# C of block 2 loaded by head pairs and turned on VectorE, the decay rows read back earlier, late stores whole

## The chip, the cores and the metric

One core of one Trainium2 chip runs the kernel. The metric is the device time of one execution in microseconds (us). The kernel before took 123.31 us in the median of three runs (123.02 to 123.41).

Five engines run their own instruction queues in order and meet through semaphores: TensorE (PE) multiplies matrices, VectorE (DVE), ScalarE (ACT) and GpSimd (POOL) work on tensors, and SyncE (SP) issues most of the transfers between memory (DRAM) and the chip's own SBUF. ACT and POOL issue some transfers too. PE writes to PSUM, which has eight banks.

## The reference, cut to what matters

A state-space scan (4 batches, 8 heads, 768 tokens, head size 32, state size 16) feeds a bilinear feed-forward layer.

```python
# per chunk of tokens, per batch and head; cum = running sum of log a within the chunk
M       = (C @ B.T) * exp(cum_i - cum_j) * causal          # tokens x tokens
y       = M @ x + (C @ state) * exp(cum_i)
state   = exp(sum log a) * state + sum_j B_j x_j exp(cum_end - cum_j)
# then, with the 8 heads side by side (256 wide):
out     = ((y @ w_a) * (y @ w_b)) @ w_out                  # 3072 x 256, f32
```

## The kernel before, in words

**Tiling.** The 768 tokens make six blocks of 128. Two batches with all their heads make a pair; a block has two pairs, so pairs 0 to 11 stand in the order of blocks, and pair p belongs to block p // 2. B and C are loaded in f32, scaled by decay factors of their tokens (a running product of `a`, over its value at the middle of the block) and cast to f16. The factor for C is that ratio, the factor for B its reciprocal, so that C @ B.T already has the decay in it.

**One pair.** `scale_bc` (L370) scales B or C of one pair on POOL, result `bm` or `cm`. `transposes` (L386) turns both to state-by-token form on PE (L409, into a PSUM bank `tr`); ACT copies B out twice (L413, `bt`) and C once (L425, `ct`). `scores` (L437) multiplies them, `mask` (L490) applies the causal mask (three quarters of a pair on DVE, L497; one quarter copied by ACT, L494, and masked by POOL, L495). `scale_x` (L357) casts x. `pv` (L555, pairs 2 and 3) or `outputs` (L583, whole blocks from block 2 on) multiplies with x and adds the state's part; `state_sums` (L646, DVE) and `state_spread` (L658, POOL: L662 or L670, then L677) carry the state from block to block.

**The other way for C.** For blocks 3 to 5 (`by_block`, L142, through `NT = 3`) C is not loaded by pairs. `load_block` (L179) issues eight transfers of 32 KB on SP, one for each of eight heads, so that four tokens of one head stand in a row of 256 bytes: tile `rq`. `scale_block` (L188) scales all four batches in one POOL instruction (L191, `mq`), and `turn_pair` (L199) turns one pair's share on DVE by 32x32 blocks (L202, `tq`). B of block 5 goes the same way. The pair loads (`load2`, L170, L174) move 128 KB in one transfer with 64 bytes in a row.

**Their factors.** `late_rows` (L319) makes the decay rows `Ps` on DVE; `store_rows` (L332, L334 on SP) writes them to DRAM, and `spread_rows` (L337, four transfers of POOL, L339) reads them back into the partitions that `load_block` uses (`Pq`); `block_factors` (L344, L345 on DVE) turns them into `fCq`. The pair-wise factors of the late blocks come straight from `Ps` by `late_factors` (L328, L330) and `fb(2)` (L826).

**The feed-forward layer.** For pairs 0 to 3, `unit(p, k)` (L726) does two of twelve slices: Wa matmuls (`aps`), a copy by ACT (`asb`, L715), Wb matmuls (`bps`), and the product on DVE (`times`, L722, `hk`). `out_half` (L755) multiplies with `w_out` (L737), ACT scales and SP stores. Whole blocks use `bunit` (L761; L769, L779) and `bout` (L785; L794, L806, stores L809 and L811).

**The order of work** is written out by hand, from L840 to the end, and each engine takes its instructions in that order. Four PSUM banks are passed around by a string, `BANKS` (L22): each call of `bank` takes the next digit, so the string says which earlier result must have been read before PE may write. The other four banks, `SC`, hold scores and pair results.

Around the change, the order is: scores of pair 2 with the state spread of pair 1 (L952); POOL then scales pair 3's B and C, reads the rows back (L971) and casts x of pair 3; the second half of pairs 0 and 1's output; transposes of pair 3; scores of pair 3 (L1030); the loads of pairs 4 to 11 on SP; units of pair 2; `pv(3)`; `block_factors` (L1048); transposes of pairs 4 and 5 (L1050, L1054), with the state sums of pair 3 and half outputs between; the scores of pairs 4 and 5 with units of pair 3; `group(2)`, block 2's outputs, and transposes of pairs 6 and 7.

Of the kernel before, what the change touches and what calls it, by code (L numbers as in the profile page):

```python
# [10 lines left out]
f32 = mybir.dt.float32  # L11
# [8 lines left out]
YS = 16.0  # L20

BANKS = (  # L22
    "0123102031203123012301230123102310231023102310231023102130213012301230210321302103123021"
    "0321032103123012032103201231023102310213201320312031203120312031203120312031203120312031"
    "2031"
)


# [1 line left out]
def kernel(  # L30
# [13 lines left out]
    nc = tc.nc  # L44

    nb, H, S, D = x.shape
    N = B.shape[-1]
    Q = 128
    NBLK = S // Q
# [5 lines left out]
    NBP = nb // 2  # L55
    NP = NBP * NBLK
    NG = NBLK - 1
    P0 = 4
    NT = 3


    j = np.arange(128)
# [21 lines left out]
    big = ctx.enter_context(tc.tile_pool(name="big", bufs=1))  # L84
# [19 lines left out]
    selr = big.tile([BH, 2, NBP, H], f32, name="selr")  # L104
    NL = NBLK - P0 // NBP
    Ps = big.tile([BH, NL, Q], f32, name="Ps")
    fBl = big.tile([128, NL, NBP * 2 * H], f32, name="fBl")
    fCl = big.tile([128, NL, NBP * 2 * H], f32, name="fCl")
    Pq = big.tile([128, NT, Q], f32, name="Pq")
    fCq = big.tile([128, NT, 4, 32], f32, name="fCq")  # L110
    fBq = big.tile([128, 4, 2 * nb], f32, name="fBq")
# [2 lines left out]
    hsx = big.tile([128, nb, NG], f32, name="hsx")  # L114
    G = big.tile([128, nb, NG], f32, name="G")

    inp = ctx.enter_context(tc.tile_pool(name="inp", bufs=9))
    pre = ctx.enter_context(tc.tile_pool(name="pre", bufs=6))
    mid = ctx.enter_context(tc.tile_pool(name="mid", bufs=4))
    ffh = ctx.enter_context(tc.tile_pool(name="ffh", bufs=4))  # L120
# [17 lines left out]
    def bank(name):  # L138
        return psf.tile([128, 512], f32, name=name, tag=f"ff{next(banks)}")


    def by_block(blk, which):  # L142
        return blk >= NBLK - NT and (which == 1 or blk == NBLK - 1)

# [32 lines left out]
        )  # L177

    def load_block(eng, blk, which):  # L179
        raw = inp.tile([128, nb, 2, 4, N], f32, name="rq", tag="rq", bufs=3)  # L180
        st[("raw", blk, which)] = raw
        for m, e in itertools.product(range(4), range(2)):
            eng.dma_start(
                raw[32 * m : 32 * m + 32, :, e].rearrange("i b g n -> i b (g n)"),
                (B, C)[which][:, 2 * m + e, blk * Q : (blk + 1) * Q, :].rearrange("b (i g) n -> i b (g n)", g=4),
            )

    def scale_block(blk, which, eng):  # L188
        f = fCq[:, blk - (NBLK - NT), :, 0 : 2 * nb] if which else fBq
        m_ = pre.tile([128, 4, nb, 2, N], f16, name="mq", tag="mq", bufs=2)  # L190
        eng.tensor_tensor(  # L191
            out=m_.rearrange("p g b e n -> p (b e) g n"),
            in0=st[("raw", blk, which)].rearrange("p b e g n -> p (b e) g n"),
            in1=f.rearrange("p g j -> p j g").unsqueeze(3).broadcast_to((128, 2 * nb, 4, N)),
            op=ALU.mult,
        )
        st[("scaled", blk, which)] = m_

    def turn_pair(p, which):  # L199
        blk, bp = divmod(p, NBP)  # L200
        t_ = mid.tile([128, 2, Q], f16, name="tq", tag="tq", bufs=6)
        nc.vector.transpose(  # L202
            t_.rearrange("p t (i g) -> p g t i", g=4),
            st[("scaled", blk, which)][:, :, 2 * bp : 2 * bp + 2].rearrange("p g t e n -> p g t (e n)"),
        )
        st[("turned", p, which)] = t_
        if which:
            st.setdefault(p, {})["CT"] = t_
# [116 lines left out]
    def last_factors():  # L325
        nc.vector.reciprocal(fBq, fCq[:, NT - 1, :, 0 : 2 * nb])

    def late_factors():  # L328
        for c0 in range(0, Q, 32):
            nc.vector.transpose(fCl[c0 : c0 + 32], Ps[:, :, c0 : c0 + 32])  # L330

    def store_rows(eng):  # L332
        rows = far.tile([BH, NT, Q], f32, name="rows")
        eng.dma_start(rows, Ps[:, NL - NT :])  # L334
        return rows

    def spread_rows(eng, rows):  # L337
        for m in range(4):
            eng.dma_start(  # L339
                Pq[32 * m : 32 * m + 2 * nb],  # L340
                rows.rearrange("(b h) k q -> b h (k q)", h=H)[:, 2 * m : 2 * m + 2],
            )

    def block_factors():  # L344
        nc.vector.transpose(  # L345
            fCq.rearrange("p k g j -> p (k g) j"), Pq.rearrange("p k (i g) -> p k g i", g=4)
        )
# [310 lines left out]
    def state_spread(p):  # L658
        blk, bp = divmod(p, NBP)
        if p + NBP < P0:  # L660
            Sbd = mid.tile([128, 2, H * D], f16, name="sbd", tag="sbd")
            nc.gpsimd.tensor_tensor(  # L662
                out=Sbd.rearrange("p t (m c) -> p t m c", m=4),
                in0=U32[:, p].unsqueeze(2).broadcast_to((128, 2, 4, 2 * D)),
                in1=maskbd.rearrange("p (m e) d -> p m (e d)", e=2).unsqueeze(1).broadcast_to((128, 2, 4, 2 * D)),
                op=ALU.mult,
            )
        else:
            Sbd = mid.tile([128, 2, 2 * D], f16, name="spair", tag="spair")
            nc.gpsimd.tensor_tensor(  # L670
                out=Sbd.rearrange("p t (e d) -> p t e d", e=2),
                in0=U32[:, p].rearrange("p t (e d) -> p t e d", e=2),
                in1=par.unsqueeze(1).unsqueeze(3).broadcast_to((128, 2, 2, D)),
                op=ALU.mult,
            )
        if blk + 1 < NG:
            nc.gpsimd.tensor_tensor(  # L677
                out=gU[:, (p + NBP) % (2 * NBP)],
                in0=U32[:, p],
                in1=G[:, 2 * bp : 2 * bp + 2, blk + 1].unsqueeze(2).broadcast_to((128, 2, 2 * D)),  # L680
                op=ALU.mult,
            )
        st.setdefault(("S", p + NBP), {})["Sbd"] = Sbd
# [29 lines left out]
    def evac_a(a_ps, on_dve=False):  # L713
        asb = ffh.tile([128, 512], f32, name="asb", tag="asb", bufs=5)
        (nc.vector.tensor_copy if on_dve else nc.scalar.copy)(asb, a_ps)  # L715
        return asb
# [9 lines left out]
    def unit(p, k2, between=None, ps=(None, None)):  # L726
        a_ps = unit_mm(p, k2, Wa, ps[0])
        asb = evac_a(a_ps)
        if between:
            between()  # L730
        b_ps = unit_mm(p, k2, Wb, ps[1])
        return lambda: times(p, k2, b_ps, asb)
# [22 lines left out]
    def out_half(p, bt):  # L755
        o_ps = bank("ops")
        out_mm(p, bt, o_ps, range(NK))
        out_store(p, bt, o_ps)
# [26 lines left out]
    def bout(blk, c, parts=1):  # L785
        bt, j = divmod(c, NBP)
        hk = st[("FF", blk)]["hk"]
        rows = out[(2 * j + bt) * S + blk * Q :][0:Q]
        w = d_model // parts
        for part in range(parts):  # L790
            o_ps = bank("ops")
            cs = slice(part * w, part * w + w)
            for k in range(NK):
                nc.tensor.matmul(  # L794
                    o_ps[:, 0:w],
                    hk[:, k, c * Q : (c + 1) * Q],
                    Wo[:, k, cs],
                    start=(k == 0),
                    stop=(k == NK - 1),
                    skip_group_check=True,  # L800
                )
            o_sb = outp.tile([128, d_model], f32, name="osb", tag="osb")
            if parts > 1 and part == 0:
                nc.vector.tensor_scalar(o_sb[:, 0:w], o_ps[:, 0:w], 1.0 / (YS * YS), None, ALU.mult)
            else:
                nc.scalar.activation(out=o_sb[:, 0:w], in_=o_ps[:, 0:w], func=AF.Copy, scale=1.0 / (YS * YS))  # L806
            if parts == 1 and (blk == NBLK - 2 or (blk == NBLK - 1 and c < 2)):
                for hs_ in (slice(0, w // 2), slice(w // 2, w)):
                    nc.sync.dma_start(rows[:, hs_], o_sb[:, hs_])  # L809
            else:  # L810
                (nc.sync, nc.scalar)[part].dma_start(rows[:, cs], o_sb[:, 0:w])  # L811

    def loads_bc(p, eng=None):
        if p < NP:
# [10 lines left out]

    def fb(k):  # L826
        if k * NBP >= P0:
            nc.vector.reciprocal(fBl[:, 0 : NL - 1], fCl[:, 0 : NL - 1])
        else:
            nc.vector.reciprocal(fB[:, k], f_c(k))  # L830

    def go(*items):
        for p, k2 in items:
            unit(p, k2)()
# [93 lines left out]
    rows = store_rows(nc.sync)  # L928
# [23 lines left out]
    def scores2():  # L952
        scores(2)
        mask(product(2, 3), by_pool=True)
        state_spread(1)

    h = unit(1, 4)
    scores2()
# [9 lines left out]
        out_mm(c // 2, c % 2, o[c], range(6))  # L968
    scale_bc(3, 0, nc.gpsimd)
    scale_bc(3, 1, nc.gpsimd)  # L970
    spread_rows(nc.gpsimd, rows)  # L971
    scale_x(3, nc.gpsimd)
    late_factors()
    fb(2)
# [5 lines left out]
    state_sums(2)  # L980
    h = unit(2, 0, lambda: transposes(3, apart=True))
    h()
    h = unit(2, 1)

    def prep(p, spread=()):
# [59 lines left out]
    go((2, 2), (2, 3), (2, 4))  # L1045
    pull(3)
    pv(3)
    block_factors()  # L1048
    go((2, 5))
    transposes(4)  # L1050
    state_sums(3)
    state_spread(3)
    out_half(2, 0)
    transposes(5)  # L1054
    prep_x(4)
# [131 lines left out]
```

## Time and profile before

| what | before |
|---|---|
| median of three runs | 123.31 us (123.02 to 123.41) |
| the profiled execution | 122.88 us, its span 121.2 us |
| granted PE clock | 0.999 |
| DVE, ACT, POOL busy | 92.8, 76.6, 65.8 us |
| DMA packets | 46,017, of them 40,000 under 512 B |
| PE's wait for the first weights ends | 12.87 us |
| last ACT instruction ends, and the store that it issues | 118.65 us, issued at 118.68 |

A row of a timeline gives start and length in us, the engine, the line, the operation, out<-in by the program's names, shapes, and in brackets the idle time before it and what ended it. Names with a q (SPq) are instructions that only issue transfers. The chain gives start and length in us of merged pieces, followed back from the last instruction of all. An "aps" or "bps" piece of the units is 0.44 us, four matmuls.

### The profile page before, as it was taken

The page shows a single profiled execution, that of the slowest core. Times are in us where ns is not written, and L with a number is a line of the kernel's source. Part 1 is how long each engine was busy: PE and PEld are TensorE (multiplying, and loading weights), DVE is VectorE, ACT ScalarE, POOL GpSimd, SP SyncE. Part 2 cuts the span into 40 slices and gives each one's busy share as a digit, 9 for nine tenths or more (in the row PEclk, how much of TensorE's full clock was granted, in tenths as well). Part 3 has the DMA queues.
Part 4 walks back from the last instruction along what each step waited for, and adds up shares of the span by engine and source line. Part 5 has one row for each costly group of instructions (what it writes and reads, how often), then busy time and mean ns, then how long its engine had stood idle before and what let it go on. Part 6 is the DMA issues. An engine that isn't in the chain of part 4 may idle for free.

```text
span 121.2 us, 3718 instructions
## 1 busy us (share of the span) xinstructions
PE 116.0 (96%) x1440; PEld 79.5 (66%) x1440; DVE 92.8 (77%) x183; ACT 76.6 (63%) x157; POOL 65.8 (54%) x92
## 2 busy tenths in 40 slices
PE   6999799999999999999999999999999999999990
PEld 2356699889898898645476464766464684555890
DVE  4999999895886979699995999996898444847100
ACT  0458866927669955987759657757666737566220
POOL 7995999479994994075999199228044000000000
PEclk9999999999999999999999999999999999999999
DMA  3999979968969279289328981011101012010122
GB/s 62 187 171 219 210 159 211 144 105 129 102 72 161 58 86 138 57 107 156 76 53 165 293 294 49 0 49 46 43 0 43 5 43 87 0 43 5 43 87 87
DMA packets 46017, 12.25 MB, mean 101 GB/s; under 512 B 40000, under 2 KB 45568, under 8 KB 46000
## 3 DMA queue, kind: packets, MB, share of 16 engines
q1 hardware_dynamic: 41344, 7.62, 32.8%
q0 software_dynamic: 2384, 3.98, 17.3%
q10 hardware_dynamic: 2272, 0.43, 1.9%
q8 instruction: 11, 0.18, 0.6%
q14 instruction: 6, 0.05, 0.2%
HBM read 11.18 MB, written 3.19 MB: 119 GB/s over the span
## 4 chain that ended last, share of the span: by engine, by line
PE 87%; DMA 5%; POOL 4%; issue 0%; ACT 0%; DVE 0%
PE ops L794 18%; PE aps L769 17%; PE bps L769 17%; PE ops L737 9%; PE aps L691 8%; PE bps L691 8%; DMA Wb<-in_moe_w_b_dram 5%; PE SC L443 2%; PE SC L503 2%; PE bps L704 1%; POOL bn L165 1%; POOL cn L165 1%; PE tr L409 1%; PE SC L518 1%; POOL Wa L213 1%; PE SC L593 1%
## 5 line engine op out<-in xcount | busy, mean ns | idle before, releaser
L715 ACT COPY asb<-aps 128x512 f32<-128x512 f32 x71 | 41.6, 589 | 13.2 <-PE aps L769 9.1
L779 DVE TENSOR_TENSOR hkb<-bps,asb 128x512 f16<-128x512 f32 x48 | 31.9, 687 | 10.3 <-ACT asb L715 9.8
L769 PE MATMUL aps<-XB,Wa 128*128 128x512 f16 x96 | 28.6, 379 | 0.0
L769 PE MATMUL bps<-XB,Wb 128*128 128x512 f16 x96 | 28.5, 379 | 0.0
L794 PE MATMUL ops<-Wo,hkb 128*128 128x256 f16 (+1 forms) x204 | 22.6, 267 | 0.0
L794 PEld LDWEIGHTS <-hkb 128*128 128x128 f16 x204 | 18.5, 98 | 3.0
L497 DVE TENSOR_TENSOR t<-SC,causal_q 128x512 f16<-128x512 f32 x24 | 15.5, 680 | 3.2 <-PE SC L443 3.2
L722 DVE TENSOR_TENSOR hk<-bps,asb 128x512 f16<-128x512 f32 x24 | 15.9, 686 | 2.1 <-ACT asb L715 1.5
L769 PEld LDWEIGHTS <-Wb 128*128 128x128 f16 x96 | 9.9, 103 | 10.9
L495 POOL TENSOR_TENSOR t<-tmp,causal_q 128x512 f16<-128x512 f32 x8 | 9.2, 1160 | 13.8 <-ACT tmp L494 13.6
L769 PEld LDWEIGHTS <-Wa 128*128 128x128 f16 x96 | 9.7, 103 | 9.0
L368 POOL TENSOR_SCALAR x<-xn 128x512 f16<-128x512 f32 x8 | 11.9, 1492 | 2.4 <-PE aps L769 1.9
L806 ACT ACTIVATE osb<-ops 128x256 f32<-128x256 f32 (+1 forms) x16 | 6.0, 378 | 11.2 <-PE ops L794 11.2
L691 PE MATMUL bps<-X2T,Wb 128*128 128x256 f16 x84 | 12.4, 273 | 0.0
L691 PE MATMUL aps<-X2T,Wa 128*128 128x256 f16 x80 | 11.9, 274 | 0.0
L737 PE MATMUL ops<-Wo,hk 128*128 128x256 f16 x96 | 11.6, 273 | 0.0
L737 PEld LDWEIGHTS <-hk 128*128 128x128 f16 x96 | 9.0, 98 | 1.2
L497 DVE TENSOR_TENSOR t<-SC,causal 128x512 f16<-128x512 f32 x13 | 8.2, 683 | 1.0 <-PE SC L458 0.8
L691 PEld LDWEIGHTS <-Wb 128*128 128x128 f16 x84 | 8.6, 103 | 0.5
L691 PEld LDWEIGHTS <-Wa 128*128 128x128 f16 x84 | 8.3, 104 | 0.7
L494 ACT COPY tmp<-SC 128x512 f32<-128x512 f32 x11 | 6.6, 597 | 1.9 <-PE SC L443 1.1
L267 PE MATMUL SC<-warm 128*128 128x512 f16 (+1 forms) x14 | 5.2, 530 | 1.0 <-POOL warm L238 1.0
(113 smaller groups left out, 139.7 us busy)
## 6 DMA issues: line engine op xcount, KB each, us to landing
out_dram<-osb SPq DMA_DIRECT2D x17, 128.0 KB, 3.4
xn<-in_x_dram SPq DMA_DIRECT2D x5, 256.0 KB, 4.4
out_dram<-osb SPq DMA_DIRECT2D x13, 64.0 KB, 1.6
Wo<-in_moe_w_out_dram POOLq DMA_DIRECT2D x2, 384.0 KB, 6.1
bn<-in_B_dram SPq DMA_DIRECT2D x6, 128.0 KB, 3.9
rq<-in_C_dram SPq DMA_DIRECT2D x24, 32.0 KB, 2.3
xn<-in_x_dram POOLq DMA_DIRECT2D x3, 256.0 KB, 4.9
xn<-in_x_dram SPq DMA_DIRECT2D x4, 128.0 KB, 4.9
```

Source lines behind the costliest of these rows:

```text
L368: eng.tensor_scalar(xo, xi, XS, None, ALU.mult)
L494: nc.scalar.copy(tmp, i_)
L495: nc.gpsimd.tensor_tensor(out=o_, in0=tmp, in1=c_, op=ALU.mult)
L497: nc.vector.tensor_tensor(out=o_, in0=i_, in1=c_, op=ALU.mult)
L691: nc.tensor.matmul(ps[:, kk * 2 * Q : (kk + 1) * 2 * Q], w_up(W, k, f), X2T[:, p, :, f], start=(f == 0), stop=(f == 1), skip_group_check=True,
L715: (nc.vector.tensor_copy if on_dve else nc.scalar.copy)(asb, a_ps)
L722: nc.vector.tensor_tensor(out=s["hk"][:, 2 * k2 : 2 * k2 + 2, :].rearrange("p k q -> p (k q)"), in0=b_ps, in1=asb, op=ALU.mult)
L737: nc.tensor.matmul(o_ps[:, 0:d_model], hk[:, k, bt * Q : (bt + 1) * Q], Wo[:, k, :], start=(k == 0), stop=(k == NK - 1), skip_group_check= ...
L769: nc.tensor.matmul(t_, w_up(W, k, f), XB[:, blk - P0 // NBP, f].rearrange("p t j q -> p (t j q)"), start=(f == 0), stop=(f == 1), skip_gro ...
L779: return lambda: nc.vector.tensor_tensor(out=s["hk"][:, k], in0=ps[1], in1=asb, op=ALU.mult)
L794: nc.tensor.matmul(o_ps[:, 0:w], hk[:, k, c * Q : (c + 1) * Q], Wo[:, k, cs], start=(k == 0), stop=(k == NK - 1), skip_group_check=True,)
L806: nc.scalar.activation(out=o_sb[:, 0:w], in_=o_ps[:, 0:w], func=AF.Copy, scale=1.0 / (YS * YS))
```

## The change

- `NT` is 4, so block 2 joins the blocks whose C is loaded by `load_block`, scaled by `scale_block` and turned by `turn_pair`. The decay rows stored, read back and turned grow from three blocks to four (`Ps` from 384 to 512 columns). Pairs 4 and 5 lose their C transfers, two POOL scalings, four PE transposes and two ACT copies; two `turn_pair` are added to DVE's order.
- `spread_rows` moves ahead of `state_spread(1)` in POOL's order, and that behind the scaling of pair 3's B and C.
- `block_factors` moves from behind `pv(3)` to behind the first unit of pair 2.
- The late blocks' pair-wise factors shrink by one block (`fBl`, `fCl`, `late_factors`).
- The tile `rq` has four buffers for three, `xn` eight for nine.
- Stores of the last two blocks that were issued in two halves are issued whole.
- `BANKS` is another string. Up to the fortieth digit it is the same; after that, by which earlier result each bank held, it differs in two places: the Wb matmuls of unit (2,4) take the bank of unit (2,3)'s Wa result and the Wa matmuls of unit (2,5) that of unit (2,2)'s Wb result, where before it was the other way round.

```diff
-    NT = 3
+    NT = 4
...
-    fBl = big.tile([128, NL, NBP * 2 * H], f32, name="fBl")
-    fCl = big.tile([128, NL, NBP * 2 * H], f32, name="fCl")
+    fBl = big.tile([128, NL - 1, NBP * 2 * H], f32, name="fBl")
+    fCl = big.tile([128, NL - 1, NBP * 2 * H], f32, name="fCl")
...
-    inp = ctx.enter_context(tc.tile_pool(name="inp", bufs=9))
+    inp = ctx.enter_context(tc.tile_pool(name="inp", bufs=8))
...
-        raw = inp.tile([128, nb, 2, 4, N], f32, name="rq", tag="rq", bufs=3)
+        raw = inp.tile([128, nb, 2, 4, N], f32, name="rq", tag="rq", bufs=4)
...
-            nc.vector.transpose(fCl[c0 : c0 + 32], Ps[:, :, c0 : c0 + 32])
+            nc.vector.transpose(fCl[c0 : c0 + 32], Ps[:, 0 : NL - 1, c0 : c0 + 32])
...
-            if parts == 1 and (blk == NBLK - 2 or (blk == NBLK - 1 and c < 2)):
-                for hs_ in (slice(0, w // 2), slice(w // 2, w)):
-                    nc.sync.dma_start(rows[:, hs_], o_sb[:, hs_])
-            else:
-                (nc.sync, nc.scalar)[part].dma_start(rows[:, cs], o_sb[:, 0:w])
+            (nc.sync, nc.scalar)[part].dma_start(rows[:, cs], o_sb[:, 0:w])
...
-            nc.vector.reciprocal(fBl[:, 0 : NL - 1], fCl[:, 0 : NL - 1])
+            nc.vector.reciprocal(fBl, fCl)
...
     def scores2():
         scores(2)
         mask(product(2, 3), by_pool=True)
-        state_spread(1)
+        spread_rows(nc.gpsimd, rows)
...
     scale_bc(3, 0, nc.gpsimd)
     scale_bc(3, 1, nc.gpsimd)
-    spread_rows(nc.gpsimd, rows)
+    state_spread(1)
     scale_x(3, nc.gpsimd)
...
     h = unit(2, 0, lambda: transposes(3, apart=True))
     h()
+    block_factors()
     h = unit(2, 1)
...
     pull(3)
     pv(3)
-    block_factors()
+    turn_pair(4, 1)
     go((2, 5))
     transposes(4)
     state_sums(3)
     state_spread(3)
+    turn_pair(5, 1)
     out_half(2, 0)
     transposes(5)
```

More of the change, by code (lines that the diff above doesn't have):

```diff
@@ L22 @@
 BANKS = (
-    "0123102031203123012301230123102310231023102310231023102130213012301230210321302103123021"
-    "0321032103123012032103201231023102310213201320312031203120312031203120312031203120312031"
-    "2031"
+    "0123102031203123012301230123102310231023103210321032103120312013201320310231203102132031"
+    "0231023102132013023102301321032103210312301230213021302130213021302130213021302130213021"
+    "3021"
 )
```

## The prediction

> **What bounds the kernel now.** I read the engine totals first, then the chain that ended last in order of time, and then, for 24 to 50 us where the change acts, the timelines of SP's DMA issues, POOL and DVE.
>
> ```profile
> PE 116.0 (96%) x1440; PEld 79.5 (66%) x1440; DVE 92.8 (77%) x183; ACT 76.6 (63%) x157; POOL 65.8 (54%) x92
> PE 87%; DMA 5%; POOL 4%; issue 0%; ACT 0%; DVE 0%
> ```
>
> TensorE (PE) is busy 96% of the span, and the chain is PE's own instructions from 12.87 us (the first weights) to 118.37 us. No other engine ends a wait of PE in between. So a change gains only what it takes out of PE's instruction stream, and it loses whatever it makes PE wait. These are the pieces of the chain around the change:
>
> ```profile
> 36.32 0.44 PE bps L691 x4
> 36.75 0.22 PE tr L409 x4
> 36.98 1.31 PE ops L737 x12
> 38.29 0.22 PE tr L409 x4
> 38.51 0.34 PE SC L443 x16
> ...
> 46.92 0.22 PE tr L409 x2
> 47.14 1.31 PE ops L737 x12
> 48.45 0.11 PE tr L409 x2
> ```
>
> "tr x4" is B and C of pair 4 (then 5) turned on PE; "x2" is pair 6 or 7, whose C VectorE (DVE) turns already. So the change makes two "x4" into "x2".
>
> **PE.** Four transposes go. Four cost 0.22 us in the chain, 0.055 us each, so -0.22 us. This is the only term that can shorten the chain. The Trainium skill ("VectorE: DVE Perf Modes", section "The three transpose paths") gives 390 ns for a TensorE transpose of 128x128; four would be an estimated 1.56 us. The chain's row is a seventh of that, and it decides.
>
> **ACT and the stores.** Two copies of C out of PSUM go (0.37 and 0.38 us). Nothing in the chain waited for them: 0. The twelve half stores become six whole ones: SP spends 0.33 us on a whole one against 0.33 + 0.42 on two halves, but it sat 15.1 us waiting for ACT ahead of those halves, and the last transfer is another, issued by ACT at 118.68. So 0, and no more than the 0.42 either way.
>
> **DVE.** The rows that matter:
>
> ```profile
> 29.87 0.69 DVE L722 TENSOR_TENSOR hk<-bps,asb 128x512 f16<-128x512 f32 x1
> 31.14 0.69 DVE L497 TENSOR_TENSOR t<-SC,causal 128x512 f16<-128x512 f32 x1 [0.58 <-PE SC L458]
> 33.57 0.69 DVE L722 TENSOR_TENSOR hk<-bps,asb 128x512 f16<-128x512 f32 x1
> 34.44 0.69 DVE L722 TENSOR_TENSOR hk<-bps,asb 128x512 f16<-128x512 f32 x1 [0.18 <-ACT asb L715]
> 35.92 0.88 DVE L345 STREAM_TRANSPOSE fCq<-Pq 128x384 f32<-128x384 f32 x1
> ```
>
> block_factors moves from 35.92 to behind the product of 29.87, and grows to 512 columns: 0.88 x 512/384 = 1.17 us, so 30.5 to 31.7. The 0.58 us of idle time before 31.14 covers half; the mask of pair 3 starts about 0.55 us later, and the product of unit (2,1) behind it ends near 33.0 instead of 32.4. Its bank is next written by the Wa matmuls of unit (2,3), which stand at 33.29 in the chain, so 0.3 us are to spare. The new bank string differs in reuse at one place only: unit (2,4)'s Wb matmuls (34.60) take the bank that ACT copied from 33.82 to 34.41, and no longer that of the product at 33.57, which would now end near 34.7. The idle 0.18 us before 34.44 and the place that block_factors leaves bring DVE back by 36. The two new transposes cost 0.74 us each (the row of the eight like them): one takes the place that block_factors leaves, the other the 0.78 us that DVE sat before the mask at 38.88. late_factors falls by a quarter of 1.24 us, in front of 1.22 us of idle time. Sum 0; if the covers were gone, 0.3 for the longer block_factors and 1.5 for the two transposes.
>
> **POOL.**
>
> ```profile
> 24.82 1.16 POOL L662 TENSOR_TENSOR sbd<-U,maskbd 128x512 f16<-128x512 f32 x1
> 28.29 2.39 POOL L339 DMA_DIRECT2D Pq<-rows  x4
> 33.46 0.62 POOL L379 TENSOR_TENSOR cm<-cn,fCl 128x256 f16<-128x256 f32 x1
> 45.52 0.62 POOL L379 TENSOR_TENSOR bm<-bn,fBl 128x256 f16<-128x256 f32 x1
> 46.66 0.62 POOL L379 TENSOR_TENSOR bm<-bn,fBl 128x256 f16<-128x256 f32 x1 [0.52 <-DMA bn<-in_B_dram]
> ```
>
> The four readbacks (2.39 us of POOL) now start at 24.85, ahead of the spread (1.16 + 0.40). Their source landed at 22.76, so they wait for nothing. Pair 3's B and C are scaled from 27.25 (27.08 now, held by a transfer), which PE needs at 29.10. The spread ends near 30.1; PE reads it at 35.04. Then x of pair 3 starts 0.65 us earlier. Two scalings of C (2 x 0.62) become one of 1.10. All this is 0.
>
> The added wait is on DVE: block_factors waits for the readbacks, and behind it stand the pair's masks and products. The last of four issues starts near 26.65; from issue to landing they took 2.4 to 3.5 us, so 29.1 to 30.2, just ahead of 30.5.
>
> **SP, the doubtful term.** SP issues the loads one after another:
>
> ```profile
> 26.98 0.95 SPq L174 DMA_DIRECT2D cn<-in_C_dram  x1
> 27.97 1.48 SPq L174 DMA_DIRECT2D bn<-in_B_dram  x1
> 29.63 1.54 SPq L174 DMA_DIRECT2D cn<-in_C_dram  x1
> 31.21 2.00 SPq L174 DMA_DIRECT2D bn<-in_B_dram  x1
> 33.25 3.15 SPq L174 DMA_DIRECT2D xn<-in_x_dram  x2
> 36.44 5.91 SPq L183 DMA_DIRECT2D rq<-in_C_dram  x8
> ```
>
> The two "cn" (2.57 us with the gaps behind them) go, and eight "rq" of 32 KB come ahead of both "bn" and all that follows. An rq issue took 0.43 us in the median (0.475 with its gap), so eight take at least 3.8 us; the row above says 5.91. SP would thus be 1.2 to 3.3 us later. But the long issues look like waiting for the queue to drain: the same 128 KB of B took 0.43 us at 42.39 and 2.00 at 31.21. With the two cn, 4,096 pieces of 64 bytes leave the queue, and the rq bring 1,024 of 256. In the trace, packets of 64 bytes go at some 1,200 per us from 32.0 to 35.3 (4,007, about those of the second cn and bn), beginning for that second cn at 31.9. If the eight are issued by 31.3 (3.8 us and one longer issue), B of pair 4 starts to flow near 32.3. I take **+0.4 us** for everything behind it, and keep 0 and 3.3 as the ends.
>
> Who waits? B of pair 4 has over 1 us to spare (landing near 34.6, needed by POOL before 36). B of pair 5 landed at 35.79 and may land at 37.4. The rq themselves land 2 to 2.6 us after the last issue, at 33 to 35; POOL is free at 32.9, its 1.10 us end by 36 at worst, and the first transpose on DVE stands at 35.9 (behind it wait the product of unit (2,5) and pair 3's state sums; behind POOL's scaling, B of both pairs). B of pair 6 is the tight one: landed at 45.45, used by POOL at 45.52, needed by PE's "tr x2" at 46.92, which now comes 0.22 earlier. With 0.62 us of work, the slack is about 0.45 us. So +0.4 is just covered; I charge 0.1 for that. Beyond, PE waits microsecond for microsecond.
>
> The Trainium skill ("DMA: Bandwidth & Descriptors", section "Rules for kernel authors") advises to join small transfers, since under 64 KB one pays mostly overhead. That speaks against eight of 32 KB for two of 128 KB, and it is the slower rival's side; the trace leans to it in issue time (3.8 against 2.57) and away from it in packets.
>
> The smaller edits cost nothing: the Pq fill (0.38 to about 0.5 us) stands before 0.72 us of idle time; x of pair 8 takes a buffer that ACT read at 7.54, long before its load at 53.59; the fifth C buffer set waits for pair 4's, used up by 38.
>
> **Sum.** -0.22 + 0.1 = -0.1 us. The profiled execution took 122.88 us (span 121.2), which gives 122.8; the median shown is 123.31, so I forecast **123.2 us**. About 0.3% (0.37 us) is what a measurement of this kernel can tell from no change.
>
> **Rivals.** (1) Slower: SP stays late. If the eight issues cost 5 us and the drain gives nothing back, B of pair 6 is 1.2 us late or more; POOL's scaling and PE's "tr x2" at 46.92 wait some 0.75 us, net +0.5: 123.8. At the upper end (3.3 us) it would be B of pair 5 that decides first, and with pair 6 the loss is near 2.5 us. It decides from 0.45 us of lateness. For it: the issue times; against: the pieces taken out of the queue. Chance 0.25.
> (2) The readbacks land late and block DVE. At 4.6 us from issue to landing (the row store's own time) they land at 31.25, block_factors ends at 32.4, the product of (2,1) at 33.7, and PE waits 0.45 us at 33.29: net +0.2, 123.5. It decides from about 30.8. Against: their own 2.4 to 3.5. Chance 0.06.
> (3) Faster by more than 0.37 us: there is no PE wait to remove, so only a shift of the runs of this size (they range from 123.02 to 123.41) or something unseen could give it, say 122.8. Chance 0.08. My forecast has 0.61.
>
> **How the numbers follow.** Faster 0.08; slower is rival 1 and a part of rival 2 with scatter, 0.28; within 0.3% the rest, 0.64. The range runs from 122.8 (-0.22 with the scatter of the runs) to 124.1 (rival 1 with 1.5 us of lateness).
>
> **What would show it.** Right: two "tr x2" of 0.11 near 36.7 and 38.2, no gap in PE's chain at 33.3 or 46.9, and the first load of block 3's C issued by SP near 36.8. Wrong: POOL idle on B of pairs 5 or 6 with PE waiting behind it, DVE idle before block_factors, or half a microsecond gone from PE's time elsewhere.

## The result, and the profile after

The changed kernel took 123.75 us (median of 22 runs, 122.64 to 124.92) against 123.02 us for the kernel before (22 runs beside them, 122.82 to 126.04): a ratio of 1.0048 with an interval of 1.0026 to 1.007, so 0.6 us slower. Two runs of before (125.07 and 126.04) and one of the changed kernel (124.92) belong to a slower state and are left out of the ratio. I had forecast no change, so the direction was wrong. That the time itself, 123.75, lies in the range is partly luck: the forecast was built on 123.31, the median of three runs of the kernel before, which 22 runs put at 123.02. The runs of the changed kernel also lie further apart (half of them between 123.35 and 124.09, against 122.93 and 123.30 for before), and the fastest of them, 122.64, beats the fastest of before. The profiled execution took 124.36 us (span 122.6).

The engine totals and the shares of the chain, from the page of the changed kernel:

```profile
PE 116.6 (95%) x1436; PEld 79.2 (65%) x1436; DVE 94.0 (77%) x185; ACT 76.4 (62%) x155; POOL 65.9 (54%) x91
PE 50%; SPq 16%; DMA 11%; POOL 9%; DVE 6%; issue 4%; ACTq 1%; ACT 1%; DVEq 0%; POOLq 0%
```

PE still has most of the span, with four instructions fewer. But it had 87% of the chain and now has 50%: the chain that ended last leaves PE and runs through SP's issues, a transfer and POOL. The chain in order of time shows where it returns to PE (start us, us, what):

```profile
43.65 0.43 SPq L174
44.09 0.04 issue
44.13 4.42 DMA bn<-in_B_dram
48.55 0.07 issue
48.62 0.63 POOL bm L379
49.25 0.05 issue
49.29 0.28 PE tr L409 x2
```

SP issues B of pair 7 at 44.13 (42.87 before), it lands at 48.55 (46.59 before), POOL scales it at once, and PE turns it at once: no step has any time to spare. The waits of PE between 24 and 80 us, of the same execution (who waited for what: us in total, times, longest; the view leaves out waits under 0.15 us):

```profile
PE tr L409 <- POOL bm L379: 0.4, 2, 0.2
PE SC L409 <- POOL cm L379: 0.3, 1, 0.3
PE SC L503 <- POOL t L495: 0.2, 1, 0.2
```

PE waits at four places: for pair 3's C (29.64), for B of pairs 6 and 7 (47.51, 49.29), and for a mask of POOL's (77.92). The profile of the kernel before has no such row in that stretch. SP's issues, and POOL's rows:

```profile
27.67 3.94 SPq L183 DMA_DIRECT2D rq<-in_C_dram  x8
31.65 2.55 SPq L174 DMA_DIRECT2D bn<-in_B_dram  x2
34.25 2.65 SPq L174 DMA_DIRECT2D xn<-in_x_dram  x2
36.94 6.67 SPq L183 DMA_DIRECT2D rq<-in_C_dram  x8
```

```profile
24.69 2.39 POOL L339 DMA_DIRECT2D Pq<-rows  x4
28.96 0.62 POOL L379 TENSOR_TENSOR cm<-cn,fC 128x256 f16<-128x256 f32 x1 [1.00 <-DMA cn<-in_C_dram]
...
35.36 1.10 POOL L191 TENSOR_TENSOR mq<-rq,fCq 128x512 f16<-128x512 f32 x1 [1.45 <-DVE hk L722]
36.42 0.62 POOL L379 TENSOR_TENSOR bm<-bn,fBl 128x256 f16<-128x256 f32 x1
...
37.72 0.62 POOL L379 TENSOR_TENSOR bm<-bn,fBl 128x256 f16<-128x256 f32 x1
...
46.83 0.62 POOL L379 TENSOR_TENSOR bm<-bn,fBl 128x256 f16<-128x256 f32 x1 [0.42 <-DMA bn<-in_B_dram]
48.62 0.62 POOL L379 TENSOR_TENSOR bm<-bn,fBl 128x256 f16<-128x256 f32 x1 [1.17 <-DMA bn<-in_B_dram]
```

The eight issues took 3.94 us and B of pair 4 was issued at 31.65. POOL scales C of block 2 ("mq") from 35.36 and B of pairs 4 and 5 behind it. The releaser named at 35.36 had long been done (it ends at 33.35): POOL waited there for the eight loads, the last of which landed at 34.62.

These are the rows that the change moved or added on DVE:

```profile
31.07 1.11 DVE L345 STREAM_TRANSPOSE fCq<-Pq 128x512 f32<-128x512 f32 x1
36.51 0.75 DVE L202 STREAM_TRANSPOSE tq<-mq 128x256 f16<-128x256 f16 x1
38.62 0.74 DVE L202 STREAM_TRANSPOSE tq<-mq 128x256 f16<-128x256 f16 x1
```

None of the three has idle time in front of it, and no PE wait names them. (Of DVE's 6% of the chain, 3% are the masks of L497.)

**Slack.** One execution shows where PE waited in it, not where it nearly did. So I read the slack of B from each trace: the start of PE's first "tr" of a pair, less the end of POOL's scaling of that pair's B (us). PE starts some 0.06 us after what it waits for, so 0.06 means none is left.

```
                         pair 4  pair 5  pair 6  pair 7
before                    1.93    1.58    0.71    1.01
x1_stores                 2.48    2.14    0.78    1.63
y1_stores_same_count      1.26    0.57    0.06    0.24
changed, first profile    0.16    0.28    0.06    0.06
changed, a1_again         0.07    0.20    0.52    0.70
changed, a2_again         0.06    0.19    0.10    0.07
changed, c1_after_again   0.06    0.06    0.06    0.19
```

x1 and y1 are experiments told below. They differ from the kernel before in how some output stores are issued, the first of them at 71 us, and in nothing else, so up to there they are two more profiles of its order. The changed kernel has 0.3 or less at pairs 4 and 5 in all of its four profiles, where the order of before has 0.57 or more in three. At pairs 6 and 7 the changed kernel mostly has none, but this alone does not set it apart: y1 has 0.06 and 0.24 there. In y1's profile, which is the slowest of its twelve runs (123.86), PE waits at two of the places where the changed kernel's does, for pair 3's C and for B of pair 6, without the change:

```profile
PE SC L409 <- POOL cm L379: 0.5, 1, 0.5
PE tr L409 <- POOL bm L379: 0.5, 1, 0.5
```

So a wait at these places in one profile does not yet show that the change made it.

### The profile page after: what moved, and what is told of

Same layout as the page of the kernel before. It is cut to its first block, busy times and chain, and to the rows that moved or that the text cites. A ratio compares the mean times of both kernels' runs of the same rounds, so it can differ in the third digit from the quotient of the medians.

```text
span 122.6 us, 3713 instructions
## 1 busy us (share of the span) xinstructions
PE 116.6 (95%) x1436; PEld 79.2 (65%) x1436; DVE 94.0 (77%) x185; ACT 76.4 (62%) x155; POOL 65.9 (54%) x91
## 4 chain that ended last, share of the span: by engine, by line
PE 50%; SPq 16%; DMA 11%; POOL 9%; DVE 6%; issue 4%; ACTq 1%; ACT 1%; DVEq 0%; POOLq 0%
PE ops L794 16%; PE aps L769 14%; PE bps L769 13%; SPq L183 8%; DMA Wo<-in_moe_w_out_dram 5%; SPq L174 5%; SPq L165 4%; DMA bn<-in_B_dram 4%; DVE t L497 3%; POOL t L495 3%; DMA cn<-in_C_dram 3%; PE SC L443 1%; DVE hkb L779 1%; POOL x L368 1%; POOL bn L165 1%
## 5 line engine op out<-in xcount | busy, mean ns | idle before, releaser
L497 DVE TENSOR_TENSOR t<-SC,causal_q 128x512 f16<-128x512 f32 x24 | 15.5, 681 | 3.1 <-PE SC L443 3.1
L497 DVE TENSOR_TENSOR t<-SC,causal 128x512 f16<-128x512 f32 x13 | 8.2, 682 | 0.3 <-PE SC L458 0.3
L202 DVE STREAM_TRANSPOSE tq<-mq 128x256 f16<-128x256 f16 x10 | 7.4, 742 | 0.0
```

Source lines behind the costliest of these rows:

```text
L202: nc.vector.transpose(t_.rearrange("p t (i g) -> p g t i", g=4), st[("scaled", blk, which)][:, :, 2 * bp : 2 * bp + 2].rearrange("p g t e ...
L497: nc.vector.tensor_tensor(out=o_, in0=i_, in1=c_, op=ALU.mult)
```

## The experiments

Theories, by letter. **A**: the eight small loads make SP late, so B of pairs 6 and 7 comes late. **B**: the readbacks, moved ahead, share the transfers with pair 3's C loads. **C**: POOL scales C of block 2, which waits for the last of the eight loads, ahead of B of pairs 4 and 5. **L** came up on the way: the number of transfers of SP and ACT sets what the end of the kernel costs.

**x1_stores** is the kernel before with whole late stores, **x2_readback** the kernel before with the readbacks ahead, **x3_two_of_eight** the changed kernel with two of the eight loads (C of six heads of block 2 is left out), **x5_extra_issues** the kernel before with five more loads of 32 KB on SP.

```diff
 # x2_readback, in scores2() and behind pair 3's scaling
-        state_spread(1)
+        spread_rows(nc.gpsimd, rows)
...
-    spread_rows(nc.gpsimd, rows)
+    state_spread(1)
 # x3_two_of_eight, in load_block, on a tile that is filled with zeros
+            if blk == 2 and m:
+                continue
 # x5_extra_issues, ahead of the loads of pair 4
+    for r in range(5):
+        nc.sync.dma_start(spare[...], C[:, r, 2 * Q : 3 * Q, :].rearrange(...))
```

> The kernel before with whole late stores as the only edit. Theory A (the eight small loads make SP late, so that B of pairs 6 and 7 and x of pair 7 land late) and theory B (the readbacks of the decay rows, moved ahead, meet pair 3's C loads and make PE wait at 29.6 us) both expect no change: ratio 0.999 to 1.001, the last store landing where it did. If the stores matter, 0.3 us either way.

> The kernel before with the four readbacks ahead of the state spread of pair 1 as the only edit (three blocks of rows, the turning of the rows left where it was). Theory A: no change, ratio 0.999 to 1.001, SP's queue as before. Theory B: C of pair 3 lands 0.5 to 1 us later than in the kernel before, POOL's scaling of it waits, PE has a gap of 0.3 to 0.5 us ahead of pair 3's second transposes; ratio 1.003 to 1.004.

> The changed kernel with two of the eight C loads of block 2; the rest of that tile is filled with zeros early on, so C of six heads of block 2 is left out. SP reaches B of pair 4 and all behind it some 2.8 us earlier. Theory A: the PE gaps at 47.5, 49.3 and 77.9 us go, 0.9 to 1.1 us of this profile; ratio 0.997 to 1.000. Theory B: only the gap at 29.6 us counts and stays; ratio 1.003 to 1.005.

> The kernel before with five more 32 KB loads on SP (of C, into a part of a tile that is written only at 94 us) ahead of pair 4's loads; nothing else changes. SP is 2.4 us later, less what the queue drains meanwhile. Theory A: B of pairs 6 and 7 land 1 to 2.4 us later, PE waits for them, 0.5 to 2 us in all; ratio 1.004 to 1.016. Theory B: below 0.2 us; ratio under 1.002.

Measured, against 123.07 us before: x1 123.43 (1.0035, interval 1.0019 to 1.0052); x2 123.23 (1.0019, 0.9998 to 1.0039); x3 123.26 (1.0013, 0.9995 to 1.003); x5 124.71 (1.015, 1.0111 to 1.0189).

x5 shows the direction of A: five more small loads cost 1.6 us. In its profile PE waits for pair 5's B at 39.21; at pairs 6 and 7, the ones that A names, the slack is 0.10 and 0.06. x2 is inconclusive by its interval; its profile has this wait of PE, between two turnings of pair 3:

```profile
28.62 0.27 PE L409 MATMUL SC<-ident,bm 128*128 128x128 f16 x2
29.55 0.28 PE L409 MATMUL SC<-ident,cm 128*128 128x128 f16 x2 [0.65 <-POOL cm L379]
```

x1 was a surprise: fewer stores, 0.36 us slower. The last store's issue, by ACT, stands at 119.01 of a span of 121.9:

```profile
119.01 0.38 ACTq L807 DMA_DIRECT2D out_dram<-osb  x1
```

That is 2.87 us from the last issue to the end, where the kernel before has 2.50 (118.68 to 121.18). The transfer took as long in both; what differs lies behind its landing, 1.28 us against 0.91. x1 and x3 issue 90 transfers on SP and ACT, the kernels before and after 96. The DMA records name eight completion semaphores that these transfers take in turn; the last store has the last of the eight where there are 96, the second where there are 90. x5, with 101, has the fifth, and 1.09 us behind the landing. That fits an end that waits for the eight one after another, some 0.06 us each: theory L. By it, x1 and x3 would have paid 0.37 us for their count alone.

**y1_stores_same_count** and **y2_two_same_count** test that: whole late stores with six earlier ones in halves (96 transfers), and x3 with the late stores in halves (96 transfers).

```diff
 # y1_stores_same_count, kernel before
-            if parts == 1 and (blk == NBLK - 2 or (blk == NBLK - 1 and c < 2)):
+            if parts == 1 and (blk == 3 or (blk == 2 and c < 2)):
```

> The kernel before with the late stores whole and six earlier stores (block 2's first two, block 3's four) in halves instead, so that SP and ACT issue 96 transfers as in the kernel before, and not 90. Theory L (the end of the kernel waits for the eight completion semaphores one after another in a fixed order, and the count of transfers decides which of them the last store has): the last store has the last semaphore again, the time from its landing to the end is 0.91 us and not 1.28, ratio 0.999 to 1.001. Theory S (whole stores themselves are slower at the end): ratio 1.003 to 1.004 as with the whole stores alone.

> The changed kernel with two of the eight C loads of block 2 (C of six heads of that block left out, zeros in their place) and the late stores in halves as before, so again 96 transfers. Theory A with L: SP early and the end short, ratio 0.996 to 0.999, the price of the late loads in the changed kernel then being about 0.8 us. If SP's lateness is not the main cause: 1.001 to 1.004.

Measured, against 122.97: y1 122.97 (1.0004, 0.9986 to 1.0021), y2 122.88 (0.9996, 0.998 to 1.0012). Behind the last landing both have 0.92 and 0.91 us. So the count sets the end, as L says, and the whole stores cost and bring nothing; that the end waits for the eight in turn is an inference from three values. y2 is the main result of the study: with two loads instead of eight and all of the change in place but the whole stores, the loss is gone. Its slack at pairs 4 to 7 is 1.66, 1.78, 0.51 and 1.36, and the one wait of PE in its profile is pair 3's (0.23 us). The loss hangs on the eight loads. What of them does it, y2 cannot say: with the six loads go SP's time, three quarters of their bytes, and POOL's wait for them. It was also not as fast as A had it (0.996 to 0.999): of the 0.22 us of the missing transposes, nothing clear of noise is left.

**y3_readback_late** puts the readbacks and the spread of the changed kernel back in the old order; C of block 2 is then scaled and turned later. **y4_b_first** is the changed kernel with B of pairs 6 and 7 ahead of C of block 3, on SP and on POOL.

```diff
 # y4_b_first
+    load2(nc.sync, 6, 0)
+    load2(nc.sync, 7, 0)
+    load_block(nc.sync, 3, 1)
...
+    scale_bc(6, 0, nc.gpsimd)
+    scale_bc(7, 0, nc.gpsimd)
+    scale_block(3, 1, nc.gpsimd)
```

> The changed kernel with the readbacks and the state spread of pair 1 in the order of before, and what hangs on them moved: the rows turned after unit (2,3), C of block 2 scaled behind B of pairs 4 and 5, pair 4's C turned after unit (2,5). SP's queue as in the changed kernel, 96 transfers. Theory B: the gap at 29.6 us shrinks, ratio 1.001 to 1.003 (late loads of B of pairs 6 and 7 stay). Theory A alone: 1.004 to 1.006, as the changed kernel. Against both stands the risk that C of pair 4 now comes late for its scores at 38.4 us: then a new PE wait there.

> The changed kernel with B of pairs 6 and 7 loaded ahead of C of block 3 on SP, and scaled ahead of it on POOL; 96 transfers, nothing taken out of SP's queue. Theory A: B of pairs 6 and 7 land 3 to 6 us earlier, PE has no gap near 47.5 and 49.3, 0.4 to 0.7 us gained: ratio 0.999 to 1.002. If the lateness of these two does not matter in the timed runs: 1.004 to 1.006.

Measured, against 122.97: y3 123.69 (1.0066, 1.0041 to 1.0091), y4 123.84 (1.0067, 1.0041 to 1.0093).

y3 has the wait that was feared of it, and none at pair 3:

```profile
PE SC L443 <- DVE tq L202: 0.8, 1, 0.8
```

So it says nothing on B. y4 seems to speak against A alone: its slack at pairs 6 and 7 is 1.57 and 2.43 us, and yet its runs take as long as the changed kernel's. At pairs 4 and 5 it has the same 0.16 and 0.28. But it has a cost of its own. C of block 3 now comes behind B, DVE waits for it, and what ACT does behind DVE is late too (its copy to XB starts at 48.38, in a2 at 47.71):

```profile
47.33 0.75 DVE L202 STREAM_TRANSPOSE tq<-mq 128x256 f16<-128x256 f16 x1 [0.54 <-POOL mq L191]
```

Even in this profile (123.11, which is its fastest run), PE stands 0.21 us ahead of the kernel before at pair 7's transposes (48.07 against 48.28) and 0.24 behind it at 52.12 (51.88 before). So y4 does not settle what A is worth.

**a1_again** and **a2_again** are two more profiles of the changed kernel. **w1_b4_first** puts B of pair 4 ahead of the eight loads (and turns C of pair 4 a unit later), **w2_b46_first** does the same for block 3.

```diff
 # w1_b4_first; w2 also for pairs 6 and 7
-    loads_bc(4)
-    loads_bc(5)
+    load2(nc.sync, 4, 0)
+    load_block(nc.sync, 2, 1)
+    load2(nc.sync, 5, 0)
...
-    prep(4, (2,))
+    scale_bc(4, 0, nc.gpsimd)
+    state_spread(2)
+    scale_block(2, 1, nc.gpsimd)
...
-    turn_pair(4, 1)
     go((2, 5))
+    turn_pair(4, 1)
```

> The changed kernel once more, one profile. By now three theories stand. A: B of pairs 6 and 7 are late. B: C of pair 3 is late. C: POOL scales C of block 2 ahead of B of pairs 4 and 5, this waits for the last of eight loads, and PE's transposes of pairs 4 and 5 then have 0.16 and 0.28 us to spare where they had 1.93 and 1.58, so that the scatter of the loads reaches PE. In a run near 123.7 us, C expects a gap of 0.2 to 0.8 us at the transposes of pair 4 or 5 (36.6 to 39.2 us); A expects it near 47 to 49.5 alone; B near 29 alone.

> The changed kernel a third time, one profile, to see whether PE's gaps stand in the same place from run to run. Expectations as for the run before it: C a gap at pairs 4 or 5, A near 47 to 49.5, B near 29.

> The changed kernel with B of pair 4 loaded ahead of block 2's eight C loads and B of pair 5 behind them on SP; POOL scales B of pair 4 and spreads pair 2's state ahead of the scaling of C; pair 4's C turned on DVE behind unit (2,5). 96 transfers, the same work. Theory C: pair 4's transposes have over 1 us to spare again, ratio 0.998 to 1.002. A alone or B alone: as the changed kernel, 1.004 to 1.007. Risk: C of pair 4 late for its scores at 38.4 us, seen as a PE gap there.

> The kernel of w1_b4_first with the same order for block 3: B of pair 6, the eight C loads, B of pair 7, on SP and on POOL. Theories A and C both in play: 0.997 to 1.001, and below w1_b4_first if the lateness of pair 6's B costs in the timed runs. Risk: pair 6's C, turned on DVE at 47.3 us, comes late and holds DVE.

Measured, against 123.16: a1 122.95 and a2 122.63 (one run each); w1 124.1 (1.0058, 1.0034 to 1.0082); w2 123.36 (1.0025, 0.9997 to 1.0052).

a2 is the changed kernel when its loads come early: no wait of PE is named from 13 us on. At each pair's missing transposes PE gains 0.11 us on the kernel before, and 0.05 more at 41.7. At the end it is 0.24 us ahead. But it was so at 12.62 already, where its wait for the first weights ended (12.87 before), in a part that the change does not touch. What the transposes gave made up for some 0.27 us that PE had lost between the two, 0.15 of it at pair 3: PE took C there 0.26 us behind B (28.78 and 29.04), and 0.11 behind it before (28.94 and 29.05). These are its turnings of pairs 6 and 7:

```profile
46.61 0.28 PE L409 MATMUL tr<-ident,bm 128*128 128x128 f16 x2
...
48.04 0.28 PE L409 MATMUL tr<-ident,bm 128*128 128x128 f16 x2
```

In the first profile the same rows stand at 47.51 and 49.29, with idle time in front of them. So the change does take its 0.22 us out of PE's instructions; even in the fastest of its profiles that is no more than what PE loses elsewhere.

w1 gave pair 4 3.08 us of slack and did not recover anything. w2, which gives slack to the pairs of both blocks (3.07, 1.25, 1.50, 1.30), is better than w1, which was timed beside it: all twelve runs of w1 lie above w2's median. So the order in block 3 is worth something once B of pair 4 comes first. Against the changed kernel w2 is 0.4 us better in the median, but the two were not timed together and their intervals overlap; it is no better than before. Both pay for turning C of pair 4 a unit later. In w2 the turned C is ready at 38.54 and PE's scores start at 38.59; the next Wa matmuls stand 0.94 to 0.95 us behind pair 5's transposes in w2 and in both profiles of w1, and 0.54 behind them in a2. That is 0.4 us that comes with the edit itself, so w1 does not show that C alone is worth nothing.

The last six runs: **v1_pool_b** lets POOL issue B of pairs 4 and 5 and scale both ahead of C of block 2, **v2_pool_loads** only issues them there; **v3_act_b4** and **v4_act_b45** let ACT issue one or both; **c1_after_again** is the changed kernel once more, and **w1_again** a second profile of w1.

```diff
 # v1, v2: behind spread_rows; v3, v4: nc.scalar, ahead of pair 2's chain
+        load2(nc.gpsimd, 4, 0)
+        load2(nc.gpsimd, 5, 0)
...
 # v1, v4
-    prep(4, (2,))
+    scale_bc(4, 0, nc.gpsimd)
+    scale_bc(5, 0, nc.gpsimd)
+    scale_block(2, 1, nc.gpsimd)
+    state_spread(2)
```

> The changed kernel, with B of pairs 4 and 5 (two loads) issued by GpSimd right behind the four readbacks (near 27.1) instead of by SP behind the eight loads of C of block 2, and with GpSimd scaling both (2 x 0.62) in the idle time it had at 33.9 to 35.4, ahead of C of block 2; two late stores are in halves again, so that SP and ACT issue 96 transfers as before. All the work is done. Theory A (the eight loads make SP late for B of pairs 6 and 7): SP is about 2.5 us earlier from 31.7 on; slack of the PE transposes of pairs 6 and 7 grows from 0.06 to over 1; time falls from 123.75 towards before minus the four transposes, 122.7 to 122.9. Theory C (scaling C of block 2 ahead of B of pairs 4 and 5 leaves their transposes 0.16 and 0.28 of slack): the slack of pairs 4 and 5 is 1.5 or more, 122.7 to 122.9 too. Rival (the readbacks beside pair 3's C loads, or the small loads themselves): the two more transfers at 27 to 30 make it no better, pair 3's cm is late by 0.3 to 0.6, 123.5 to 124.

> As v1_pool_b, but GpSimd keeps the order of the changed kernel: C of block 2 is scaled first, then B of pair 4, later B of pair 5. SP is 2.5 us earlier as in v1, the slack of the transposes of pairs 4 and 5 stays at 0.1 to 0.3. Theory A alone: as v1, 122.7 to 122.9. Theory C alone: no gain on the changed kernel, 123.5 to 123.8. Both: between the two.

> The changed kernel itself, timed on the chip of v1 and v2, so that these are compared with it as well as with the kernel before. All theories: 1.0026 to 1.007 of the kernel before, with a scatter of over 1.5 us between its runs against 0.8 or so of the kernel before. If it comes out at 1.000 or below, what was timed first belonged to one chip and not to the kernel.

> w1_b4_first once more, for its profile alone. Its first profile lost 1.01 us at 14.3, where the third x load landed at 13.53 instead of 11.8, in a part that the edit does not touch. If that belongs to the run: no such gap, and a span near 121.3. If it belongs to the program as built: a gap of 0.5 to 1 at 14.3 again, and a span over 121.9; then w1's time says nothing on the order of B of pair 4.

> The changed kernel with B of pair 4 issued by ACT in its idle 2.0 us before pair 2's chain (near 24.6), so that SP has one load less behind the eight small ones, and with GpSimd scaling B of pair 4 ahead of C of block 2, in its idle time at 33.9 to 35.4. 96 transfers on SP and ACT as before; all the work is done. Theory A and C (the loss is slack used up: 0.16 and 0.28 us at pairs 4 and 5, 0.06 at 6 and 7): slack of pair 4 over 2, of pair 5 near 0.8, of pairs 6 and 7 some 0.5 more; 122.8 to 123.0, and runs within 1 us of each other. Theory B (traffic beside pair 3's C loads): PE's gap at 29 grows to 0.5 or more, 123.4 to 123.8.

> As v3_act_b4, with B of pair 5 issued by ACT too, and scaled by GpSimd ahead of C of block 2. Theory A and C: slack of pairs 4 and 5 over 1.5, of pairs 6 and 7 over 0.5; 122.7 to 122.9, the four removed transposes being all that is left. Theory B: two more transfers of 128 KB at 25 to 28 make pair 3's C land later than in v3; its cm is late by 0.6 to 1, 123.7 to 124.2.

Measured, against 122.92: v1 124.34 (1.0119, 1.01 to 1.0138), v2 124.68 (1.0138, 1.0099 to 1.0178), c1 123.4 (1.0032, 1.0009 to 1.0055), w1_again 123.33. Against 123.08: v3 127.19 (1.0334, 1.0312 to 1.0356), v4 123.58 (1.0043, 1.002 to 1.0065).

c1 confirms the loss against other runs of the kernel before; its profile loses 0.50 us at pair 6. w1_again has no gap at 14.3, so w1's 1.01 us there belonged to that run. Of the rest of w1's time, 0.4 us is the later turning of C.

v1 to v4 missed their numbers, each by a new wait that I had not priced. In v1, POOL's two issues took 1.20 and 1.17 us, where SP took 0.43 for such a load at 42.39 in the kernel before, and pair 3's scaling came behind them:

```profile
26.90 2.37 POOL L174 DMA_DIRECT2D bn<-in_B_dram  x2
29.29 0.63 POOL L379 TENSOR_TENSOR bm<-bn,fB 128x256 f16<-128x256 f32 x1
29.87 0.62 POOL L379 TENSOR_TENSOR cm<-cn,fC 128x256 f16<-128x256 f32 x1
```

```profile
PE SC L409 <- POOL bm L379: 1.1, 1, 1.1
PE SC L409 <- POOL cm L379: 0.3, 1, 0.3
```

In v3 and v4, ACT's issue did not go out when ACT was idle, but at 30.17, and at 26.71 and 27.37:

```profile
30.17 0.40 ACTq L174 DMA_DIRECT2D bn<-in_B_dram  x1
30.68 0.60 ACT L581 ACTIVATE X2T<-SC 128x512 f16<-128x512 f32 x1 [6.34 <-DMA rq<-in_C_dram]
```

```profile
26.71 1.89 ACTq L174 DMA_DIRECT2D bn<-in_B_dram  x2
28.70 0.60 ACT L581 ACTIVATE X2T<-SC 128x512 f16<-128x512 f32 x1 [4.19 <-PE ops L737]
```

Each of the three went out 0.02 us after a transfer of SP's with the same completion semaphore had landed (30.15, 26.69, 27.35). PE then waited 2.93 us in v3 and 0.79 in v4 for ACT's copy. That is not all of v3's 4.1 us: behind its wait PE's granted clock was 0.82 from 32 to 33 us and 0.50 from 33 to 36, and PE, 2.82 us behind the kernel before when it resumed at 31.32, was 4.37 behind at 36.08. Past the waits named, neither v1 nor v4 has another in its profile from 13 us on: slack is 0.5 or more at pairs 4 to 7, and span less the named wait is 121.0 in both (122.4 - 1.44, 121.8 - 0.79), as in a2 (120.9). That fits A and C together, but these are single profiles, and v1 and v2 do not separate A from C: their intervals overlap.

**What stands.** Shown: the loss belongs to the kernel (1.0048 and 1.0032); it goes when six of the eight loads go (y2); the changed order leaves B of pairs 4 and 5 with 0.28 us of slack or less, where the order of before had 0.57 or more; and moving B of pair 6 forward helps once B of pair 4 is forward too (w2 against w1). The waits named in the changed kernel's profiles add up to between 0 and 1.0 us, at pair 3, 6 or 7 or at a late mask, never at the same set of places.

Argued, not shown: that the lateness of SP and POOL's order are how the eight loads do it. None of the four profiles names a wait at pairs 4 and 5 (c1 comes 0.14 us late at pair 5), and y1 has waits at pairs 3 and 6 without the change. y4 and w1, which relieve one block alone, each carry a cost of 0.4 us of their own, so they exclude neither A nor C.

Open: which of the places costs the timed runs most, as they have no traces, and what share the readbacks have. x2 says between 0 and 0.5 us. The second of pair 3's C loads took 2.79, 3.41 and 3.56 us from issue to landing with the readbacks behind it (x1, y1, y3), and 3.13 to 3.98 beside them in the changed kernel's four profiles, so they may add something; y1's late C (28.46 and 28.64) came before its first readback was issued at 29.37. None of the versions that do all the work beats the kernel before.

## Why the prediction was wrong, point by point

- **PE, -0.22.** Right: at each pair's missing transposes PE gains 0.09 to 0.11 us on the kernel before, in all four profiles, so the row of 0.055 us a transpose held. (a2's 0.24 us at the end is no proof of it, as it had them before the change acts.) The Trainium skill ("VectorE: DVE Perf Modes", section "The three transpose paths") would have given an estimated 1.56 us for four; the measurement decides.
- **ACT and the stores, 0.** Right (y1), but for a reason that I did not have: the change takes six transfers away and adds six, so that the count stays at 96. The stores alone would have moved the end by 0.37 us (x1); the six loads alone were not run.
- **DVE, 0.** Right. The factors' transpose ran from 31.07 without idle time in front, and no PE wait names DVE. Rival 2 did not come: the readbacks took 3.2 to 3.9 us in the first profile, a little over the 2.4 to 3.5 that I had read, and the last was there at 29.70.
- **POOL, 0.** Wrong in two places. I counted POOL's rows and not what stands in what order. Pair 3's C landed at 28.42 and 28.82 in the first profile, beside the readbacks (28.62 to 29.70), and PE waited 0.35 us for it; how much of that is the readbacks' is open, as y1 had such a wait without them. And "B of pair 4 has over 1 us to spare" was read as the transfer's landing, when POOL cannot take it before "mq" is done. I had "its 1.10 us end by 36 at worst" and B of both pairs "behind POOL's scaling" in the text, and did not add them up: "mq" ends at 36.46, B of pair 4 behind it at 37.04, and PE's row stands at 37.20. The last load landed at 34.62, and "mq" began 0.74 us after that, a wait that I had not charged.
- **SP, +0.4 us of lateness, charged 0.1.** This is the term that failed. For SP's issues the +0.4 was near at first: block 3's first C load went out at 36.94, 36.70, 36.10 and 37.04 in the four profiles, against 36.44 before. But B of pair 6, behind that block's eight loads, went out at 43.65, 42.60, 42.84 and 43.42, against 42.39, and landed 0.4 us late in a2 (45.83 against 45.45), 0.9 in c1 (46.38) and 1.3 in the first profile (46.76). So "+0.4 is just covered" was right of the best case alone. The step also took one landing for the landing: in x1, x2 and y1, where SP issues its loads in the order of before, the same load landed at 44.42, 44.55 and 47.04. A slack of 0.45 us read from one execution covers nothing of that size, and what is not covered passes on to PE: 0.44 us of waits at pairs 6 and 7 in the first profile, 0.50 in c1, none in a1 and a2. To give the 0.6 us measured, the term would have had to be some 0.8 instead of 0.1; that figure is worked back from the result, and it takes in the waits at pair 3, which are not SP's lateness. The Trainium skill ("DMA: Bandwidth & Descriptors", section "Rules for kernel authors") speaks against transfers under 64 KB; no run here tests that, as none joins the eight, and y2, which drops six of them, drops their bytes too.
- **The rivals.** Rival 1, slower by 0.5 with SP late, came nearest, with its place (pair 6) seen in two of four profiles. I gave it 0.25. That its 123.8 met the 123.75 measured is partly luck: its eight issues were to cost 5 us and took 3.94, and its base of 123.31 was 0.3 too high. The evidence for more was in the text: 3.8 us of issues for 2.57 us, and a slack of 0.45.

## What to carry to other kernels

When a change takes time out of the bound engine and puts transfers in front of others, add up the slack of each consumer behind them, through the in-order engine that stands between the landing and the bound engine, and compare it with how far landings differ between executions; a slack that is "just covered" in one execution was a loss in the median here. Read several profiles of both kernels before naming one wait as the cause: four of the changed kernel put it at different places, and one of the old order had two of these waits too. When an experiment moves a load forward, look at what it puts behind: y4 and w1 each brought a cost of 0.4 us that way. And when an experiment changes the number of transfers, keep their count (here modulo eight) or measure the end separately.

## What the runs showed of the hardware that was not expected

- The end of the kernel depends on which of eight completion semaphores the last transfer of SP and ACT has: 0.91, 1.09 and 1.28 us from its landing to the end, for the eighth, the fifth and the second (96, 101 and 90 transfers; 96 in all profiles but those of x1, x3 and x5, with 0.90 to 0.92 us).
- In v3 and v4 ACT's three issues each waited until the last transfer with the same semaphore had landed, though SP had issued that: in v3 till 30.17, for a load that landed at 30.15. The wait holds the in-order engine: ACT's next copy came late, and PE waited 2.93 us for it.
- POOL's instruction that needs eight loads began 0.74 us after the last had landed (34.62 to 35.36; in a2 34.13 to 34.87, in c1 33.94 to 34.68). Whether two loads would have cost less, y2 does not show: they had landed at 30.35, and POOL came to them at 33.38.
- The same load of 128 KB cost 1.2 us of POOL's time to issue (v1), and 0.4 on ACT (v3).
- After PE's idle 2.93 us in v3 the granted clock was down to 0.50 for 3 us, which cost PE another 1.5 us.
- One load, issued in the same order, landed between 44.42 and 47.04 us in four profiles (before, x1, x2, y1).
